# The third MoE span by seven products, and five PSUM copies given to VectorE

## The chip, the cores and the metric

The kernel runs on one core of one Trainium2 chip. The metric is the device time of one execution in microseconds (us), from the start of the program on the core to its end. Several timed executions are made and their median is taken. Beside them stands one profiled execution, from which every duration of a single instruction in this document comes.

The core's engines work from instruction queues of their own, each in order: TensorE (PE in the profile, its weight loads apart as PEld), VectorE (DVE), ScalarE (ACT), GpSimd (POOL) and SyncE (SP), which here issues DMAs. They wait for one another through semaphores.

## The reference

The kernel computes a blockwise causal attention and feeds its result to a small MoE block with a maximum of two projections as its activation. Cut to what matters:

```python
B, H, S, D = 8, 8, 576, 64
scores = (1/sqrt(D)) * q @ k^T            # masked in blocks of 64, block_i >= block_j
attn   = softmax(scores)
x      = (attn @ v) as [B*S, H*D]         # 4608 tokens x 512
h1, h2 = x @ w1, x @ w2                   # 512 -> 1024
out    = maximum(h1, h2) @ w_out          # 1024 -> 512, float32, 4608 x 512
```

The kernel uses max(h1, h2) = h2 + relu(h1 - h2). With d = w1 - w2, g = relu(x @ d) and M = w2 @ w_out, the output is y = x @ M + g @ w_out. So a row block of y is a sum over twelve chunks of 128: four of x against M and eight of g against w_out.

## The kernel before, in words

**Attention.** The 64 heads are taken in 32 pairs `p`, two pairs to a group `g` and four pairs to a batch of 576 tokens. For a pair, TensorE makes scores (L536, L554) into PSUM, ScalarE takes the exponential into SBUF (L560, L616), GpSimd zeroes the masked corners (L565), and TensorE multiplies by v (L644, tile `ps_o`). VectorE divides by the sum (reciprocal L650, multiplication L651 into `xp`). The result is transposed into `xT`, from the third batch on by a DMA transpose issued by SP (L662). K is cast by a GpSimd DMA (`kb`, L138) and transposed by another DMA of SP (L147, `kT`), from group 6 on; q is loaded by SP (L121), cast on GpSimd (L161), transposed on TensorE (L517) and copied out of PSUM, one head pair by VectorE and the other by ScalarE (L525).

**MoE.** The tokens are cut into ten spans: two small ones for the first batch, then spans 2 to 9 of 512 tokens (the last 448). Per span, eight units (`h_unit`) make x @ d for 128 of the 1024 columns, with four matmuls of 512 columns each (L244), and `g` is written by the relu. In spans below `FAST` VectorE does every relu (L252); from `FAST` on ScalarE does the odd ones (L250).

Then y is made in one of two ways:

- Spans below `FAST` (0, 1 and 2) use `y_unit`: for each 128 tokens, twelve matmuls of 512 columns into one bank of PSUM (L291), one VectorE copy out (L296), one store of SP (L297). Span 2 has four such units, 48 matmuls.
- Spans from `FAST` on use seven products in place of eight half-size ones, a scheme of Strassen's kind. A span is two row halves of 256 tokens, x|g is cut into two halves of the twelve chunks, and the weights M|w_out into two column halves of 256. Sums of halves are formed first: `weight_sums` (L354, eight instructions in all, once per kernel) and `row_sums` (L360, eight per span). A product is twelve matmuls of 256 columns (L386, tile `ps_p`), so a span has 84. `after` combines the products: the first is copied out of PSUM to a tile `u` (L411, on ScalarE), the others are added by VectorE (L415, L420, L426, L431, L435, L437, L440). SP stores the four quarters (L405).

The order of the products is (1, 2, 6, 5, 4, 7, 3) for all spans but the last one.

**What sets the order.** The order of every engine's instructions is written out by hand: instructions are issued in the order in which the Python code runs, and each engine takes its own in that order. MoE work is cut into generators (`units`), and `fill(n)` issues about n matmuls' worth of it between pieces of attention. Which unit comes next is decided by order in the list and by whether the tokens it needs are done (`done_tokens`). `fill_of(g)` spreads the ready work evenly over the groups. The main loop runs over groups, with two pairs each, and each pair does: MoE work, attention of pair p-2 in two parts around a few matmuls (`av_with`: `ps_o` of two tiles, fill, `ps_o` of three tiles), transposes of q, scores of the next tiles, GpSimd work, then one `weight_sums` for p = 10 to 17.

**PSUM.** The scores have four banks of eight. Everything else (`ps_h`, `ps_y`, `ps_p`, `ps_o`, `ps_qT`) shares the other four, in pool `ps_m`: a matmul that opens a new tile waits until the former tile in its bank has been read. In the steady groups the bank of product 1 goes next to the three-tile `ps_o` that follows the second product.

Of the kernel before, what the change touches and what calls it, by code (L numbers as in the profile page):

```python
# [14 lines left out]
def kernel(  # L15
# [57 lines left out]
    NSPAN = len(spans)  # L73


    FAST = 3
    carry = [t0 % P for t0, _ in spans]
    tiles = [(carry[i] + w) // P for i, (_, w) in enumerate(spans)]

# [31 lines left out]
    dve, pool, act = nc.vector.tensor_copy, nc.gpsimd.tensor_copy, nc.scalar.copy  # L111
# [88 lines left out]
    dve, pool, act = nc.vector.tensor_copy, nc.gpsimd.tensor_copy, nc.scalar.copy  # L200
# [30 lines left out]
    def h_unit(i, f):  # L231
# [11 lines left out]
        for c in range(NDM):  # L243
# [4 lines left out]
            if c == NDM - 1:  # L248
                if i >= FAST and on_act(i, f):
                    nc.scalar.activation(out=g[:, f, m:m + w], in_=pt[:, :w], func=AF.Relu)  # L250
                else:
                    nc.vector.tensor_scalar_max(g[:, f, m:m + w], pt[:, :w], 0.0)  # L252
                if i >= FAST and f in X_SUMS:
                    row_sums(i, X_SUMS[f], 0)
            yield

    def bT_unit(j):
        pt = ps_m.tile([P, 2, NDM, P], BF16, name="ps_bT", tag="m")
        for i in range(2):
            for c in range(NDM):  # L260
                nc.tensor.transpose(pt[:, i, c, :], w2_sb[j][:, c, i * P:(i + 1) * P], ident[:])
                if i == 1 and c == NDM - 1:
                    (act if j % 2 else dve)(
                        out=bT_sb[:, 2 * j:2 * j + 2, :],
                        in_=pt.rearrange("p i c d -> p i (c d)"))
                yield
# [65 lines left out]
    def b_parts(half, col):  # L332
        cs = slice(col * HN, (col + 1) * HN)
        return m_sb[:, 2 * half:2 * half + 2, cs], wo_sb[:, 4 * half:4 * half + 4, cs]

    def t_parts(n):
        return slot[n][:, 0:2], slot[n][:, 2:6]
# [8 lines left out]
    def weight_sums(n):  # L346
        m, op, x, y = (
            (1, sub, (0, 1), (0, 0)), (3, sub, (1, 1), (0, 1)),
            (2, add, 3, (0, 0)), (4, sub, (1, 0), 2))[n // 2]
        if not slot:  # L350
            for k in range(1, 5):
                slot[k] = wraw.tile([P, 8, HN], BF16, name="sums", tag="w1raw")
        get = lambda z: b_parts(*z) if isinstance(z, tuple) else t_parts(z)
        op(t_parts(m)[n % 2], get(x)[n % 2], get(y)[n % 2])  # L354

    def row_sums(i, n, k):
        op, x, y = (
            (add, (1, 0), (1, 1)), (sub, 1, (0, 0)), (sub, (0, 0), (1, 0)), (sub, (0, 1), 2))[n - 1]
        get = lambda z: a_parts(i, *z) if isinstance(z, tuple) else s_parts(i, z)
        op(s_parts(i, n)[k], get(x)[k], get(y)[k])  # L360
# [8 lines left out]
    def on_act(i, f):  # L369
        return i >= 8 or f % 2  # L370

    def product(i, n, cuts=((0, 0, HN), (1, 0, HN))):
        for m in G_SUMS.get(n, ()):
            row_sums(i, m, 1)
        lhs = chunks({1: lambda: a_parts(i, 0, 0), 2: lambda: a_parts(i, 0, 1), 4: lambda: a_parts(i, 1, 1)}.get(
            n, lambda: s_parts(i, {3: 4, 5: 1, 6: 2, 7: 3}[n]))())
        rhs = chunks({1: lambda: b_parts(0, 0), 2: lambda: b_parts(1, 0), 3: lambda: b_parts(1, 1)}.get(
            n, lambda: t_parts({4: 4, 5: 1, 6: 2, 7: 3}[n]))())
        st = part_sums.setdefault(i, {})
        pt = None  # L380
        for k, (s, m, w) in enumerate(cuts):
            if pt is None or len(cuts) > 2:
                pt, p0 = ps_m.tile([P, 2 * HN if len(cuts) == 2 else w], FP32, name="ps_p", tag="m"), s * HN + m
            q0 = s * HN + m - p0
            for c in range(6):
                nc.tensor.matmul(  # L386
                    pt[:, q0:q0 + w], lhs[c][:, s * P:(s + 1) * P], rhs[c][:, m:m + w],
                    start=(c == 0 and q0 == 0), stop=(c == 5 and q0 + w == pt.shape[1]),
                )
                if c == 5 and q0 + w == pt.shape[1]:  # L390
                    after(i, n, st, pt, p0, q0 + w)
                yield

    def after(i, n, st, pt, p0, w):
        new = lambda: y_pool.tile([P, d_model], FP32, name="y")
        t0 = spans[i][0] - carry[i]

        def store(t, row, col):
            r0 = t0 + 2 * row * P
            if w < d_model:  # L400
                s, m = divmod(p0, HN)
                nc.sync.dma_start(
                    out=out[r0 + s * P:r0 + (s + 1) * P, col * HN + m:col * HN + m + w], in_=t[:, p0:p0 + w])
                return
            nc.sync.dma_start(  # L405
                out=out[r0:r0 + 2 * P, col * HN:(col + 1) * HN].rearrange("(s p) d -> p s d", p=P),
                in_=t.rearrange("p (s d) -> p s d", s=2))

        if n == 1:
            st["u"] = new()  # L410
            act(out=st["u"][:], in_=pt[:])  # L411
        elif n == 2:
            if i < NSPAN - 1:
                st["c"] = new()
                add(st["c"][:], pt[:], st["u"][:])  # L415
            else:
                add(st["c"][:, p0:p0 + w], pt[:], st["c"][:, p0:p0 + w])
            store(st["c"], 0, 0)
        elif n == 6 and i < NSPAN - 1:
            add(st["u"][:], pt[:], st["u"][:])  # L420
        elif n == 6:
            st["c"], st["u"] = st["u"], new()
            add(st["u"][:], pt[:], st["c"][:])
        elif n == 5:
            st["v"] = new()
            add(st["v"][:], pt[:], st["u"][:])  # L426
            if 4 in st:
                add(st["u"][:], st[4][:], st["u"][:])
        elif n == 4:
            if "v" in st:  # L430
                add(st["u"][:], pt[:], st["u"][:])  # L431
            st[4] = pt
        elif n == 7:
            t = new()
            add(t[:], pt[:], st["v"][:])  # L435
            store(t, 1, 1)
            add(st["u"][:], pt[:], st["u"][:])  # L437
            store(st["u"], 1, 0)
        elif n == 3:
            add(st["v"][:], pt[:], st["v"][:])  # L440
            store(st["v"], 0, 1)
# [6 lines left out]
    def plan():  # L448
        def h(i, f):
            t0, w = spans[i]  # L450
            units.append((h_unit(i, f), t0 + w, w / SPAN, NDM))

        def y(i, s, last=False):
            t0, w = spans[i]
            if last:
                units.append((y_last(i, s), t0 + w, 0.333, 3 * NY))
            else:
                units.append((y_unit(i, s), t0 + w, 1.0, NY))

        for i in range(NSPAN):  # L460
            for f in range(NFF):
                h(i, f)
                if i > FAST and f < 7:
                    units.append((product(i - 1, ORDER[f]), spans[i - 1][0] + spans[i - 1][1], 0.5, NY))
                if i == 0 and f % 2:
                    units.append((bT_unit(f // 2), 0, 0.25, 2 * NDM))
                if 2 < i <= FAST and f % 2 == 0 and f // 2 < tiles[i - 1]:
                    y(i - 1, f // 2)
# [230 lines left out]
    def fill_of(g):  # L699
        if g == NG - 1:  # L700
            return 45
        left = 5 - g if g < 5 else 2 - (g - 5) % 2
        return -(-max(0, ready() - KEEP) // left)
# [146 lines left out]
    for g in range(GPB + 1, NG):  # L850
        a, b = 2 * g, 2 * g + 1
        old = done_tokens[0]
        if x_due:
            x_out(x_due.pop())
        n, new = fill_of(g), done_tokens[0]
        region(tile_0(a), tile_1(a))
        lo, hi = max(3, n // 18), n * 2 // 9
        for p, tiles in ((a, lambda: (tile_2(a), tile_0(b))), (b, lambda: (tile_1(b), tile_2(b)))):
            done_tokens[0] = old if p == a and x_by_dma(g - 2) else new
            fill(hi)  # L860
            av_with(p - LAG, lo)
            done_tokens[0] = new
            if p % 2 and x_by_dma(g - 1):
                x_dma(g - 1)
            if p % 2 == 0:
                for nm in "qk":
                    if g + 1 < NG and by_dma(nm, g + 1):
                        transpose_blocks(nm, g + 1)
            copy_out = t_pair(p)
            outs = tiles()  # L870
            copy_out()
            region(*outs)
            if p % 2 and g + 1 < NG:
                pad_keys(p + 1)
                pad_keys(p + 2)
            pool_work(p)
            if 0 <= p - 10 < 8:
                weight_sums(p - 10)
        x_due.append(g - 1)
        fill(n - 2 * (lo + hi))  # L880
    for p in range(NPAIR - LAG, NPAIR):
# [48 lines left out]
```

## Time and profile before

| | |
|---|---|
| median of 3 timed executions | 253.36 us (253.33 to 253.37) |
| profiled execution: its time | 254.14 us |
| its span, first to last instruction | 252.2 us |
| PE busy | 238.7 us, 95% |
| DVE busy | 172.1 us, 68% |
| ACT busy | 143.4 us, 57% |
| POOL busy | 129.3 us, 51% |
| granted TensorE clock | 1.00 throughout |

The profiled execution takes 0.78 us more than the median, and 1.94 us of it lie around the span. Differences are worked out within it and then applied to the median.

In the middle of the kernel the work repeats once per batch (two groups). In the trace such a stretch runs from one block of five `ps_h` matmuls to the next: 70.60 to 96.06 us (the stretch in which y of span 2 is made), 96.06 to 121.32, 121.32 to 146.58, 146.58 to 171.84 (spans 3, 4 and 5), and 171.84 to 195.68 us (span 6, with less attention left to prepare). In the timeline, a row is one group of like instructions: start, duration to the end of the last one, engine, line, tiles, count, and in brackets how long the engine stood idle before it and what released it. Matmuls overlap: a row's duration has the tail of its last matmul in it, so the distance between the starts of two rows tells the pace.

### The profile page before, as it was taken

How to read it: one execution, taken by the hardware profiler on the slowest of the kernel's cores; microseconds unless marked ns; L12 is line 12 of the kernel's file. 1: busy time of each engine (PE TensorE's matmuls, PEld its weight loads, DVE VectorE, ACT ScalarE, POOL GpSimd, SP SyncE). 2: the span in 40 equal slices, each digit the busy share in tenths (PEclk: the TensorE clock that was granted, in tenths of full speed). 3: DMA queues.
4: the chain of work that ended last, by engine and by line, in shares of the span. 5: the costliest groups of instructions: out<-in, count | busy, mean ns of one | idle time of the engine just before them, and what ended most of it. 6: DMA issues, size and time to landing. Idle time of an engine off the chain costs nothing.

```text
span 252.2 us, 7449 instructions
## 1 busy us (share of the span) xinstructions
PE 238.7 (95%) x3037; PEld 160.2 (64%) x3037; DVE 172.1 (68%) x371; ACT 143.4 (57%) x200; POOL 129.3 (51%) x294
## 2 busy tenths in 40 slices
PE   8699899799999999999999999999999999999992
PEld 2347667656555555577657765776578568567782
DVE  4876986657496638786678567856785788526573
ACT  2788864575673738673867386748674650362200
POOL 1996952479759385938493849384622220010000
PEclk9999999999999999999999999999999999999999
DMA  7999999579899999999999899999993321301205
GB/s 241 317 220 310 192 270 225 215 61 198 176 134 251 158 187 171 213 111 185 246 217 157 162 208 114 203 138 220 156 154 70 109 55 44 125 0 44 91 34 170
DMA packets 107842, 41.32 MB, mean 164 GB/s; under 512 B 89248, under 2 KB 100640, under 8 KB 107808
## 3 DMA queue, kind: packets, MB, share of 16 engines
q0 software_dynamic: 65952, 11.87, 61.6%
q1 hardware_dynamic: 41584, 28.39, 50.7%
q8 instruction: 24, 0.39, 0.8%
q10 hardware_dynamic: 272, 0.59, 0.7%
q14 instruction: 10, 0.08, 0.1%
HBM read 34.60 MB, written 9.44 MB: 175 GB/s over the span
## 4 chain that ended last, share of the span: by engine, by line
PE 71%; ACT 10%; DMA 6%; DVE 6%; POOL 3%; issue 2%; SPq 0%; ACTq 0%; DVEq 0%; POOLq 0%
PE ps_p L386 21%; PE ps_h L244 19%; PE ps_y L291 9%; PE ps_o L644 8%; PE ps_s L536 7%; ACT aT L560 6%; PE ps_w L506 4%; DMA kraw<-in_k_dram 4%; DMA qraw<-in_q_dram 3%; DVE bT_sb L360 2%; ACT g L250 2%; PE ps_qT L517 2%; PE ps_M L272 1%; POOL kn L161 1%; DVE y L435 1%
## 5 line engine op out<-in xcount | busy, mean ns | idle before, releaser
L560 ACT ACTIVATE aT<-ps_s 128x1024 bf16<-128x1024 f32 (+2 forms) x100 | 95.7, 994 | 35.4 <-PE ps_s L536 26.3
L244 PE MATMUL ps_h<-xT,d_sb 128*128 128x512 bf16 (+3 forms) x320 | 69.4, 358 | 0.3 <-DVE d_sb L191 0.3
L565 POOL MEMSET aT<- 64x128 bf16 x124 | 22.0, 200 | 58.3 <-ACT aT L560 57.3
L244 PEld LDWEIGHTS <-d_sb 128*128 128x128 bf16 x320 | 29.5, 98 | 27.3 <-issue 2.3
L644 PEld LDWEIGHTS <-aT 128*128 128x128 bf16 x960 | 37.2, 98 | 10.9 <-issue 3.1
L644 PE MATMUL ps_o<-vv,aT 128*128 128x65 bf16 x960 | 39.8, 194 | 1.6 <-ACT y L411 1.6
L252 DVE TENSOR_SCALAR g<-ps_h 128x512 bf16<-128x512 f32 (+2 forms) x44 | 26.4, 605 | 13.6 <-PE ps_h L244 13.1
L165 POOL DMA_DIRECT2D vv<-in_v_dram x40 | 33.9, 854 | 1.3 <-issue 0.9
L250 ACT ACTIVATE g<-ps_h 128x512 bf16<-128x512 f32 (+1 forms) x36 | 20.9, 586 | 23.2 <-PE ps_h L244 22.3
L651 DVE TENSOR_TENSOR xp<-ps_o,rec 128x256 bf16<-128x256 f32 (+1 forms) x64 | 31.4, 491 | 2.2
L536 PE MATMUL ps_s<-qT,kT 64*128 64x64 bf16 (+6 forms) x344 | 31.3, 280 | 1.6 <-ACT kT L525 0.7
L138 POOL DMA_DIRECT2D kb<-in_k_dram x40 | 29.4, 758 | 0.0
L386 PE MATMUL ps_p<-sums,bT_sb 128*128 128x256 bf16 x168 | 25.2, 273 | 0.0
L525 ACT COPY qT<-ps_qT 128x576 bf16<-128x576 bf16 (+1 forms) x17 | 10.3, 614 | 24.6 <-PE ps_qT L517 24.6
L386 PEld LDWEIGHTS <-bT_sb 128*128 128x128 bf16 x224 | 21.4, 98 | 3.4 <-issue 1.0
L650 DVE RECIPROCAL rec<-ps_o 128x4 f32<-128x4 f32 (+1 forms) x64 | 11.8, 184 | 15.1 <-PE ps_o L644 15.1
L161 POOL CAST qn<-qraw 128x1152 bf16<-128x1152 f32 (+1 forms) x16 | 17.2, 1072 | 8.7 <-DMA qraw<-in_q_dram 8.7
L536 PEld LDWEIGHTS <-kT 64*128 64x128 bf16 x344 | 12.2, 94 | 10.7 <-issue 5.0
L386 PEld LDWEIGHTS <-g 128*128 128x128 bf16 x172 | 15.6, 98 | 3.5 <-issue 1.9
L386 PE MATMUL ps_p<-wo_sb,g 128*128 128x256 bf16 (+1 forms) x116 | 17.6, 269 | 0.0
L291 PE MATMUL ps_y<-wo_sb,g 128*128 128x512 bf16 x64 | 16.7, 380 | 0.0
L236 POOL COPY g<-g 128x512 bf16<-128x512 bf16 x8 | 5.9, 732 | 20.6 <-ACT g L250 20.3
(94 smaller groups left out, 317.9 us busy)
## 6 DMA issues: line engine op xcount, KB each, us to landing
qraw<-in_q_dram SPq DMA_DIRECT2D x16, 576.0 KB, 5.2
out_dram<-y SPq DMA_DIRECT2D x35, 256.0 KB, 3.7
vv<-in_v_dram POOLq DMA_DIRECT2D x32, 128.0 KB, 6.1
kraw<-in_k_dram SPq DMA_DIRECT2D x5, 576.0 KB, 7.7
kb<-in_k_dram POOLq DMA_DIRECT2D x40, 72.0 KB, 6.9
w1raw<-in_moe_w_dram POOLq DMA_DIRECT2D x4, 512.0 KB, 7.4
xT<-in_moe_w_dram POOLq DMA_DIRECT2D x4, 256.0 KB, 7.9
wo_sb<-in_moe_w_out_dram POOLq DMA_DIRECT2D x2, 512.0 KB, 9.8
```

The costliest lines, as they stand in the source:

```text
L138: nc.gpsimd.dma_start(out=n[h * BLK:(h + 1) * BLK, :, s], in_=(q if nm == "q" else k)[b, 4 * u + 2 * s + h].rearrange("(j p) d -> p j d", ...
L165: nc.gpsimd.dma_start(out=vv_r[b % NV][P - rows:, c, :, :D], in_=v[b, :, c * P:c * P + rows, :].rearrange("h p d -> p h d"),)
L244: nc.tensor.matmul(pt[:, :w], d_sb[:, c, f * P:(f + 1) * P], xT[:, c, t0:t0 + w], start=(c == 0), stop=(c == NDM - 1),)
L250: nc.scalar.activation(out=g[:, f, m:m + w], in_=pt[:, :w], func=AF.Relu)
L252: nc.vector.tensor_scalar_max(g[:, f, m:m + w], pt[:, :w], 0.0)
L291: nc.tensor.matmul(py[:], lhs, rhs, start=(n == 0), stop=(n == len(terms) - 1),)
L386: nc.tensor.matmul(pt[:, q0:q0 + w], lhs[c][:, s * P:(s + 1) * P], rhs[c][:, m:m + w], start=(c == 0 and q0 == 0), stop=(c == 5 and q0 + w ...
L536: nc.tensor.matmul(ps[:, hh, col:col + w], kT[r, k0:k0 + P], qT[r, q0:q0 + w], start=True, stop=True,)
L560: nc.scalar.activation(out=aT_r[p % NA][:, :, a0:a0 + w], in_=ps[:, :, :w], func=AF.Exp, scale=scale,)
L565: (eng or nc.gpsimd).memset(aT_r[p % NA][BLK:, :, a0:a0 + BLK], 0.0)
L644: nc.tensor.matmul(po[:, gi, hh, :], a[:, hh, a0:a0 + P], vv[:, c, h0 + 2 * hh, :], start=(mm == 0), stop=(mm == n_mm - 1),)
L651: nc.vector.tensor_mul(xp[:, :, ts[0]:ts[0] + n, p % 2].rearrange("q s t d -> q t s d"), po[:, :, :, :D], rec[:, :n].to_broadcast([P, n, 2 ...
```

## The change

There are three edits, all in the order and placement of work; the output is the same sums.

1. `FAST` goes from 3 to 2, so span 2 is done as the later spans: y by seven products (84 matmuls of 256 columns in place of 48 of 512), the odd relus on ScalarE, eight `row_sums` and eight combining instructions on VectorE (one copy, seven additions) in place of four copies and four relus.
2. `weight_sums` is called twice per pair at p = 8 to 11, in place of once per pair at p = 10 to 17, so that the sums exist when span 2 needs them.
3. The copy of the first product out of PSUM is issued to VectorE in place of ScalarE for spans 2 to 6; for spans 7 to 9 it stays on ScalarE.

```diff
-    FAST = 3
+    FAST = 2
...
         if n == 1:
             st["u"] = new()
-            act(out=st["u"][:], in_=pt[:])
+            (dve if i < 7 else act)(out=st["u"][:], in_=pt[:])
...
             pool_work(p)
-            if 0 <= p - 10 < 8:
-                weight_sums(p - 10)
+            for i in range(2 * (p - 8), 2 * (p - 8) + 2):
+                if 0 <= i < 8:
+                    weight_sums(i)
```

In the changed program TensorE's instructions in span 2's stretch stand in the same order as in the stretches of spans 3, 4 and 5. Outside that stretch TensorE's order is as before. On VectorE the copy (L411) stands after the copy of qT (L525) and ahead of the reciprocal (L650) of the next two-tile `ps_o`. On SP the four stores of span 2 are quarters of 256 x 256 in place of 128 x 512.

## The prediction

> **What bounds the kernel now.** I read the page first: TensorE is busy for 95% of the span and carries most of the chain of waits that ended last. The question is then where TensorE stands still.
>
> ```profile
> PE 238.7 (95%) x3037; PEld 160.2 (64%) x3037; DVE 172.1 (68%) x371; ACT 143.4 (57%) x200; POOL 129.3 (51%) x294
> PE 71%; ACT 10%; DMA 6%; DVE 6%; POOL 3%; issue 2%; SPq 0%; ACTq 0%; DVEq 0%; POOLq 0%
> ```
>
> Second, the busy time by stretch: span 2's stretch (y by whole units), then those of spans 3, 5 and 6 (y by products).
>
> ```profile
> 70.60:96.06 25.46, 25.46 (x293) 13.59 (x292) 16.43 (x35) 14.03 (x19) 16.82 (x38) 1.00 1.63 185
> 96.06:121.32 25.26, 24.62 (x329) 17.23 (x328) 19.66 (x41) 16.76 (x24) 16.79 (x38) 1.00 1.79 171
> 146.58:171.84 25.26, 24.62 (x329) 17.25 (x328) 18.09 (x37) 16.73 (x24) 16.78 (x38) 1.00 1.43 164
> 171.84:195.68 23.84, 23.44 (x307) 16.48 (x306) 16.54 (x35) 15.61 (x22) 10.15 (x27) 1.00 1.15 151
> ```
>
> The first numbers are length and PE busy. Span 2's stretch has no idle TensorE at all; each later one is only 0.20 us shorter and has 0.64 us of idle in it. Third, the list of waits tells which idle that is; of TensorE's own waits in these stretches only the first and the third row are there.
>
> ```profile
> PE ps_o L644 <- ACT y L411: 1.6, 4, 0.4
> DVE y L415 <- ACT y L411: 1.4, 4, 0.4
> PE ps_qT L517 <- DVE xp L651: 0.7, 3, 0.2
> ```
>
> Fourth, the timeline around one of the four, for TensorE, ScalarE and VectorE.
>
> ```profile
> 160.22 0.38 PE L386 MATMUL ps_p<-sums,xsum 128*128 128x256 bf16 x2
> 161.00 0.90 PE L644 MATMUL ps_o<-vv,aT 128*128 128x65 bf16 x24 [0.40 <-ACT y L411]
> ...
> 159.45 1.02 ACT L560 ACTIVATE aT<-ps_s 128x1024 bf16<-128x1024 f32 x1
> 160.37 0.58 ACT L411 COPY y<-ps_p 128x512 f32<-128x512 f32 x1
> ...
> 158.68 0.75 DVE L525 COPY qT<-ps_qT 128x576 bf16<-128x576 bf16 x1
> 159.98 0.18 DVE L650 RECIPROCAL rec<-ps_o 128x4 f32<-128x4 f32 x1 [0.55 <-PE ps_o L644]
> 160.20 0.42 DVE L651 TENSOR_TENSOR xp<-ps_o,rec 128x256 bf16<-128x256 f32 x1
> 160.98 0.69 DVE L415 TENSOR_TENSOR y<-ps_p,y 128x512 f32<-128x512 f32 x1 [0.36 <-ACT y L411]
> ```
>
> Product 1 is complete at 158.88 (its last matmul starts at 158.60 and takes 0.27), but its copy stands on ScalarE behind two exponentials and starts at 160.37. The three-tile `ps_o` needs that bank. Two matmuls after 160.22, at a pace of 0.11, TensorE could have begun it at 160.44; it began at 161.00. So the stall is 0.56 us, not the 0.40 of the row, which counts from the tail of the last matmul. It is the same in the stretches of spans 3, 4, 5 and 6. By the same reading the third wait, before the transposes of q, costs 0.43 (begun at 169.75, second matmul at 170.18, where such matmuls follow one another in hundredths).
>
> Fifth, the pace of the two sorts of y matmuls.
>
> ```profile
> 86.48 1.90 PE L291 MATMUL ps_y<-wo_sb,g 128*128 128x512 bf16 x8
> 88.22 1.03 PE L291 MATMUL ps_y<-m_sb,xT 128*128 128x512 bf16 x4
> 89.08 1.46 PE L291 MATMUL ps_y<-wo_sb,g 128*128 128x512 bf16 x6
> ```
>
> From 86.48 to 89.08 are 12 matmuls: 0.217 each. In span 5's stretch the 28 matmuls of 256 columns from 162.41 to 165.48 take 0.110 each.
>
> **The change, part by part.**
>
> Edit 1, span 2 by products. TensorE: 48 x 0.217 = 10.4 us go, 84 x 0.110 = 9.2 come: 1.2 us less. The rest of the stretch stands in the order of the later ones, so it gets their 0.43 stall before the transposes (VectorE works through two additions of product 7, a reciprocal and a multiplication first): net -0.76. With the 0.56 stall too it would be -0.20, which is just the 25.46 against 25.26 of the table; the sum reproduces the stretches.
> VectorE in that stretch: four copies (0.69) and four relus (0.69) go; eight row sums (0.41 to 0.86), one copy and seven additions (0.69) come. That is span 5's load, 18.09 us of 25.26, plus about 2 us of sums. ScalarE gets four relus of 0.60: as in span 5, whose ScalarE waits for TensorE (0.48 to 1.72 us) before each pair of exponentials. Both lie beside TensorE; without that cover a relu late on ScalarE would hold a `ps_h` bank for 0.60.
>
> Here the Trainium skill has a rule against the edit. "TensorE: Matmul & The Clock Gate", section "Back-to-back issue gap", gives sustained spacings of 81 ns for 128 columns and 131 ns for 512. On a straight line that makes an estimated 98 ns for 256: 84 products' matmuls would take 8.2 us against 6.3, a loss of 1.9 in place of a gain of 1.2, and the whole change would end 0.1 us slower. The trace does not show these spacings: its rows give 110 and 217 ns, half the columns at half the time, and the measurement decides.
>
> Edit 2, the weight sums. The same eight instructions (0.41 or 0.68), two more at p = 8 and p = 9 each, and the last ones earlier. At p = 8 they start behind the copy of qT, at 59.30, and take about 0.93 at VectorE's pace; VectorE stood idle for 0.97 there until 60.34. At p = 9 the idle is 2.04 (63.2 to 65.23). At p = 10 the larger sum is new ahead of the copy of the last `ps_y`: the copy ends at 72.04 in place of 71.43, and its bank is wanted at 72.35. At p = 11 one smaller sum is new, ahead of a relu: 0.1 late, nobody waits. Cost taken: 0. The bounds: 0, and 0.8 if the sums at p = 10 ran at half pace, as the row sum at 153.14 does (0.86 in place of 0.41) while GpSimd casts q; GpSimd sets masks at that place, and the wide sums' rows are all 0.68. A gain is excluded, since no sum was waited for. Span 3's stretch loses 1.8 us of sums (19.66 against 18.09 busy); VectorE is not what ends there.
>
> Edit 3, the copy on VectorE. No row shows VectorE copying `ps_p`, but `ps_y` has the same form: 0.69, against ScalarE's 0.58. Hand over span 5: product 1 ready at 158.88, VectorE free of the qT copy at 159.35, copy until 160.04. TensorE wants the bank at 160.44: 0.40 to spare, the 0.56 stall goes. Queued behind the copy are the reciprocal and multiplication of the two-tile `ps_o`. They start at 159.98 as before, since the copy is issued in the 0.55 of idle and the pace between such instructions is 0.61. Then L415 can start at 160.55 in place of 160.98, so everything behind is earlier too. VectorE also takes over the wait for a free `y` buffer; that store was issued a stretch earlier and lands within 2 to 8 us. ScalarE loses 0.58 and only idles more. What is late next: the scores after `ps_o`, now at 161.27, need exponentials that end at 160.47; then `kT` (below).
> Gain: four stretches x 0.56 = 2.24.
>
> Queues. GpSimd issues the same DMAs and masks in the same order. On SP, span 2's four stores have the old size but stand where later spans have theirs, so the transposes of `kT` come behind the pair of stores after product 7: 1.5 us before the next block of `ps_h` (144.88 against 146.42) in place of 3.2 (92.88 against 96.06). TensorE needs `kT` 8.2 us after that issue (153.07 less 144.88). At this place the transposes landed after 5.2, 5.3 and 7.8 us; the longest of all took 9.3. Cost between 0 and (9.3 - 8.2) x 5 = 5.5 us. I take 0: three rows at this very place held. The third is close: its weight load waited 0.4 us, without holding a matmul up. A gain is excluded; no matmul waits for `kT` now.
>
> The sum: -0.76 - 2.24 = -3.00. Against the profiled execution: span 252.2 to 249.2, its time 254.14 to 251.14. That execution is 0.78 over the median, so the median goes from 253.36 to 250.36.
>
> **The rivals.**
>
> A. The copy comes late on VectorE as well, and the bank's stall stays under another name. Against it: 0.40 us to spare in a stretch whose instructions repeat to a hundredth. For it: VectorE is nearly gapless from 155.5 to 164.4, so a copy late by 1 us finds no room. With all five stalls at 0.56: 253.36 - 0.20 = 253.16, within 0.2%.
>
> B. DMA sets the pace of the stretch. For it: the DMA engines are 90% busy or more in most slices, 1.4 to 1.8 packets in flight per engine. Were each stretch held half way, -3.00 would become -1.50: 251.9. Against it: landings of 2.6 us for the transposes of x at 138 and 189 show that the backlog clears.
>
> C. Slower: the transposes of `kT` land after TensorE wants them, at the one place above, once per stretch. At the longest landing, 9.3, five stalls of 1.1 cost 5.5 and eat the 3.0: 255.9. It decides from a mean landing of 8.8 us on (0.6 of stall in each of five). For it: 2% more DMA per time, and the 7.8 row. Against it: the 5.2 and 5.3.
>
> D. The seven products do not save what the pace says, the bank's stall goes all the same: -2.24 and the new 0.43, 251.6.
>
> **How the numbers follow.** The forecast, within 0.5 of 250.4: 0.70. B or D, 251 to 252.8: 0.15. A: 0.06. C, or some other wait of VectorE that I did not see: 0.09. The upper end goes to 252.0, which takes in B and D; the lower to 249.8, since nothing but the 0.43 stalls could still go. Outside lie A, C and the worst of B, about 0.18. A measurement of this kernel can tell about 0.2% (0.5 us) from no change; faster than that: 0.70 + 0.15 = 0.85; the same: 0.06; slower: 0.09.
>
> **What would show it.** Right: the waits of `ps_o` for L411 are gone from the list; the five stretches take 24.7 us each (span 6's 23.3), with the 0.43 before the transposes in the first four as TensorE's only idle; 48 fewer `ps_y` matmuls, 84 more `ps_p`. Wrong: `ps_o` waiting for L411 on VectorE (A); weight loads or scores waiting for `kT` (B, C); the stretch of span 2 gaining less than 0.5 (D); a reciprocal that starts later after its `ps_o` than before, with `ps_qT` waiting longer.

## The result and the profile after

The changed kernel takes 250.34 us in the median (249.97 to 251.42, four executions), the kernel before, on the same chip, 253.37 us (253.33 to 253.55). The ratio is 0.9886, with a 95% interval of 0.9854 to 0.9918. In a second set of measurements (shown below as an experiment) it was 0.9877, 0.9858 to 0.9896. The forecast was 250.4 us.

The profiled execution took 251.42 us, with a span of 249.6 us. Busy time of the engines and the chain of waits that ended last, of the kernel after:

```profile
PE 234.7 (94%) x3054; PEld 163.8 (66%) x3073; DVE 179.1 (72%) x383; ACT 143.7 (58%) x200; POOL 128.9 (52%) x294
PE 79%; DMA 9%; DVE 4%; POOL 3%; ACT 2%; issue 1%; SPq 0%; POOLq 0%
```

TensorE has 4 us less to do, VectorE 7 us more, and ScalarE's part of the chain falls from 10% to 2%. The chain's DMA part grows by 5.8 us; 5.4 of them are a load of q at the start of the program, where the chain of the profile before took another path.

The stretches of the kernel after, of spans 2, 3 and 5 (length; busy time of PE, PEld, DVE, ACT, POOL; clock; DMA share; GB/s):

```profile
70.91:95.61 24.70, 24.41 (x329) 17.25 (x328) 20.43 (x43) 16.28 (x23) 16.76 (x38) 1.00 1.64 177
95.61:120.31 24.70, 24.35 (x329) 17.24 (x328) 18.55 (x38) 16.25 (x23) 16.75 (x38) 1.00 1.66 183
145.01:169.71 24.70, 24.35 (x328) 17.23 (x328) 18.55 (x38) 16.25 (x23) 16.75 (x38) 1.00 1.46 190
```

All are 24.70 us long, and span 2's stretch now has the 329 matmuls of the others. Measured alike in both traces, from the first block of `ps_h` matmuls of a span to the first block of the next, the five stretches of spans 2 to 6 take

| stretch of span | 2 | 3 | 4 | 5 | 6 | sum |
|---|---|---|---|---|---|---|
| before | 25.45 | 25.26 | 25.27 | 25.26 | 24.56 | 125.80 |
| after | 24.70 | 24.70 | 24.70 | 24.70 | 24.00 | 122.80 |

So -3.00 us between 70 and 196 us. (The stretches given ahead of the prediction begin 0.16 us behind the block's first matmul, and the last of them was ended at 195.68, where no block begins: the next one starts at 196.24. So span 6's stretch is 24.56 and not 23.84, and the 24.00 here stands against the 23.3 of the prediction.) The list of waits of the kernel after has no row of `ps_o` behind L411 any more; TensorE's row for the transposes of q behind `xp` has one occurrence more, and the early one behind the cast of q, at 47 us, is larger than the 1.3 of before:

```profile
PE ps_qT L517 <- POOL qn L161: 1.8, 1, 1.8
...
PE ps_qT L517 <- DVE xp L651: 1.0, 4, 0.2
```

That early wait is why the span of this one execution fell by 2.6 us and not by 3.0.

The timeline around the place where the stall was, now in span 2's stretch, for TensorE and then for VectorE:

```profile
83.87 0.38 PE L386 MATMUL ps_p<-m_sb,xT 128*128 128x256 bf16 x2
84.09 0.35 PE L644 MATMUL ps_o<-vv,aT 128*128 128x65 bf16 x6
84.27 0.60 PE L386 MATMUL ps_p<-wo_sb,g 128*128 128x256 bf16 x4
84.71 0.38 PE L386 MATMUL ps_p<-sums 128*128 128x256 bf16 x2
84.93 0.90 PE L644 MATMUL ps_o<-vv,aT 128*128 128x65 bf16 x24
```

```profile
83.17 0.75 DVE L525 COPY qT<-ps_qT 128x576 bf16<-128x576 bf16 x1
83.84 0.68 DVE L411 COPY y<-ps_p 128x512 f32<-128x512 f32 x1
84.47 0.18 DVE L650 RECIPROCAL rec<-ps_o 128x4 f32<-128x4 f32 x1
84.69 0.42 DVE L651 TENSOR_TENSOR xp<-ps_o,rec 128x256 bf16<-128x256 f32 x1
85.03 0.68 DVE L415 TENSOR_TENSOR y<-ps_p,y 128x512 f32<-128x512 f32 x1
```

And the same place in span 5's stretch, the one that the prediction shows with its stall:

```profile
158.81 0.38 PE L386 MATMUL ps_p<-sums,xsum 128*128 128x256 bf16 x2
159.03 0.90 PE L644 MATMUL ps_o<-vv,aT 128*128 128x65 bf16 x24
```

In span 2's stretch the copy of product 1 stands right behind the copy of qT and ends at 84.52. The three-tile `ps_o` starts at 84.93, two matmuls after 84.71, with no idle time in brackets; in span 5's stretch it is 0.22 as well (159.03 less 158.81). The reciprocal follows the copy without a gap, 0.03 us after the modelled end of its `ps_o` (84.44).

What is left of TensorE's idle time in a stretch, in the same kernel:

```profile
93.67 0.20 PE L517 MATMUL ps_qT<-ident,qn 64*128 64x64 bf16 x1
94.11 0.43 PE L517 MATMUL ps_qT<-ident,qn 64*128 64x64 bf16 x17 [0.24 <-DVE xp L651]
```

From the first transpose of q to the second are 0.44 us, where others follow in hundredths: VectorE has not yet freed the bank, behind two additions of product 7.

### The profile page after: what moved, and what is told of

The parts are those of the page before. It is cut to its first block, busy times and chain, and to the rows that moved or that the text cites. A ratio compares the mean times of both kernels' runs of the same rounds, so it can differ in the third digit from the quotient of the medians.

```text
span 249.6 us, 7510 instructions
## 1 busy us (share of the span) xinstructions
PE 234.7 (94%) x3054; PEld 163.8 (66%) x3073; DVE 179.1 (72%) x383; ACT 143.7 (58%) x200; POOL 128.9 (52%) x294
## 4 chain that ended last, share of the span: by engine, by line
PE 79%; DMA 9%; DVE 4%; POOL 3%; ACT 2%; issue 1%; SPq 0%; POOLq 0%
PE ps_p L386 29%; PE ps_h L244 22%; PE ps_o L644 9%; PE ps_s L536 9%; DMA qraw<-in_q_dram 5%; PE ps_y L291 4%; DMA kraw<-in_k_dram 4%; PE ps_qT L517 2%; PE ps_M L272 1%; ACT aT L560 1%; DVE y L435 1%; DVE y L437 1%; POOL kn L161 1%; PE ps_w L506 1%; DVE xp L651 1%
## 5 line engine op out<-in xcount | busy, mean ns | idle before, releaser
L244 PE MATMUL ps_h<-xT,d_sb 128*128 128x512 bf16 (+3 forms) x308 | 68.4, 357 | 1.0 <-DVE d_sb L191 0.3
L250 ACT ACTIVATE g<-ps_h 128x512 bf16<-128x512 f32 (+1 forms) x40 | 23.3, 587 | 23.4 <-PE ps_h L244 22.1
L252 DVE TENSOR_SCALAR g<-ps_h 128x512 bf16<-128x512 f32 (+2 forms) x40 | 23.6, 596 | 12.8 <-PE ps_h L244 12.5
L386 PE MATMUL ps_p<-sums,bT_sb 128*128 128x256 bf16 x192 | 28.9, 273 | 0.0
L386 PEld LDWEIGHTS <-bT_sb 128*128 128x128 bf16 x256 | 24.4, 98 | 3.9 <-issue 1.2
L525 ACT COPY qT<-ps_qT 128x576 bf16<-128x576 bf16 (+1 forms) x17 | 10.3, 614 | 24.5 <-PE ps_qT L517 24.5
L386 PEld LDWEIGHTS <-g 128*128 128x128 bf16 x196 | 17.7, 98 | 4.1 <-issue 2.4
L386 PE MATMUL ps_p<-wo_sb,g 128*128 128x256 bf16 (+1 forms) x132 | 20.1, 270 | 0.0
L650 DVE RECIPROCAL rec<-ps_o 128x4 f32<-128x4 f32 (+1 forms) x64 | 11.8, 184 | 9.7 <-PE ps_o L644 9.5
L360 DVE TENSOR_TENSOR bT_sb<-g 128x1024 bf16<-128x1024 bf16 x16 | 11.0, 689 | 6.6 <-ACT g L250 6.0
```

The lines of the kernel that those rows point to most:

```text
L244: nc.tensor.matmul(pt[:, :w], d_sb[:, c, f * P:(f + 1) * P], xT[:, c, t0:t0 + w], start=(c == 0), stop=(c == NDM - 1),)
L386: nc.tensor.matmul(pt[:, q0:q0 + w], lhs[c][:, s * P:(s + 1) * P], rhs[c][:, m:m + w], start=(c == 0 and q0 == 0), stop=(c == 5 and q0 + w ...
```

## The experiments

Stretches are given as in the table above, for spans 2 to 5. "Early wait" is the time that TensorE loses at about 46 us, before the transposes of q of group 4, measured by the pace like the other stalls.

**1. The copy alone.** The kernel before, with the third edit only.

```diff
-            act(out=st["u"][:], in_=pt[:])
+            (dve if i < 7 else act)(out=st["u"][:], in_=pt[:])
```

> Edit 3 alone: span 2 by whole units and the weight sums as before, the first product of spans 3 to 6 copied by VectorE. My theory: the four stalls of 0.56 us before the three-tile ps_o go and nothing else moves, so the stretches of spans 3, 4 and 5 take 24.7 us in place of 25.26, that of span 2 stays at 25.46, and the time is 253.37 - 2.24 = 251.1 (ratio 0.991). Rival A (the copy is late on VectorE too): 253.4. If the gain of the whole change came from the seven products: 253.4.

Measured: 251.18 us (250.61 to 252.11), ratio 0.9933 (0.9915 to 0.995). Stretches 25.46, 24.70, 24.70, 24.69, and span 6's 24.00: 0.56 less in each of four, nothing in span 2's. No wait of `ps_o` for L411 is left. The third edit by itself is worth 4 x 0.56 = 2.24 us in the trace. The ratio of the timed executions gives 1.7 us (1.3 to 2.2), somewhat less.

**2. Span 2 by products, the copy left on ScalarE** (edits 1 and 2).

```diff
-    FAST = 3
+    FAST = 2
...
-            if 0 <= p - 10 < 8:
-                weight_sums(p - 10)
+            for i in range(2 * (p - 8), 2 * (p - 8) + 2):
+                if 0 <= i < 8:
+                    weight_sums(i)
```

> Edits 1 and 2 without 3: span 2 by seven products, the copy on ScalarE in all spans. My theory: TensorE saves 1.19 us of matmuls in span 2's stretch but gets both stalls of the later stretches there (0.56 and 0.43), so that stretch goes from 25.46 to 25.26 and the time from 253.37 to 253.2 (ratio 0.999). If the seven products alone were worth the change: 250.3. If matmuls of 256 columns cost more than half of those of 512, as the spacings of the skill's page on TensorE would have it: 255 to 256.

Measured: 252.88 us (252.35 to 255.0), ratio 1.0002 (0.9985 to 1.002). Stretches 25.27, 25.25, 25.26, 25.27. The waits of this kernel:

```profile
PE ps_o L644 <- ACT y L411: 2.0, 5, 0.4
...
PE ps_qT L517 <- DVE xp L651: 0.9, 4, 0.2
```

There are now five stalls behind ScalarE's copy and four behind `xp`. In span 2's stretch the products save 1.2 us and bring back 0.56 and 0.43: 25.45 becomes 25.27, too little for the times to show. The first edit pays only because the third removes the stall that it would inherit: alone it is worth 0.2 us, on top of the copy 0.76.

**3. The weight sums alone** (edit 2: their earlier and denser order, with `FAST` left at 3).

> Edit 2 alone: the weight sums two per pair from p = 8, all else as before. My theory: hidden in idle time of VectorE, 253.4, ratio 1.000, and no new wait of TensorE. Rival (VectorE's queue is what ends the pairs of group 4): up to 2.2 us slower, 255.6.

Measured: 252.96 us (252.03 to 253.47), ratio 0.9992 (0.9979 to 1.0004), stretches 25.46, 25.26, 25.26, 25.27. The sums cost nothing that can be seen.

**4. The copy twice.** The changed kernel, with VectorE's copy issued two times.

```diff
         if n == 1:
             st["u"] = new()
+            if i < 7:
+                dve(out=st["u"][:], in_=pt[:])
             (dve if i < 7 else act)(out=st["u"][:], in_=pt[:])
```

> The changed kernel with the VectorE copy of the first product issued twice (same source and target) in spans 2 to 6, which doubles its cost and nothing else. My theory: the single copy ends 0.40 us before TensorE wants the bank, the second ends 0.60 to 0.68 later, so each of the five stretches gets a stall of 0.20 to 0.28 and the time goes from 250.3 to 251.4-251.8. If the copy had no slack: five times 0.6, 253.4. If it had more than 0.7: 250.3.

Measured: 251.91 us (251.1 to 252.9), ratio 0.9953 (0.9936 to 0.997), stretches 25.08, 25.08, 25.08, 25.09. The timeline of span 5's stretch, VectorE and TensorE:

```profile
157.19 0.68 DVE L411 COPY y<-ps_p 128x512 f32<-128x512 f32 x1
157.91 0.69 DVE L413 COPY y<-ps_p 128x512 f32<-128x512 f32 x1
...
158.06 0.38 PE L386 MATMUL ps_p<-sums,xsum 128*128 128x256 bf16 x2
158.65 0.91 PE L646 MATMUL ps_o<-vv,aT 128*128 128x65 bf16 x24 [0.21 <-DVE y L413]
```

The second copy starts 0.72 us after the first, not 0.61; that it waits because it writes the same tile is likely, but not shown. `ps_o` could have begun at 158.28 and began at 158.65: a stall of 0.37 in each of five stretches, somewhat more than expected, since the delay was 0.72. The other 0.35 is what the copy really had to spare (I had read 0.40). This is rival A brought about on purpose: the bank's stall returns under VectorE's name as soon as the copy is later than that.

**5. The 0.43 stalls taken away as well.** ScalarE copies product 7, and VectorE's two additions of it, with their stores, come after the third relu unit of the next span.

```diff
         elif n == 7:
             t = new()
+            if i < 7:
+                act(out=t[:], in_=pt[:])
+
+                def finish(u=st["u"], v=st["v"]):
+                    add(u[:], t[:], u[:])
+                    store(u, 1, 0)
+                    add(t[:], t[:], v[:])
+                    store(t, 1, 1)
+                later.append(finish)
+                return
...
-            add(st["v"][:], pt[:], st["v"][:])
-            store(st["v"], 0, 1)
+            z = new() if i < 7 else st["v"]
+            add(z[:], pt[:], st["v"][:])
+            store(z, 0, 1)
...
             if c == NDM - 1:
+                if f == 2 and later:
+                    later.pop()()
```

> The changed kernel with product 7 of spans 2 to 6 copied out of PSUM by ScalarE, and its two additions on VectorE moved behind the third relu unit of the next span (from SBUF; product 3's sum gets a tile of its own). My theory: the 0.43 us stall before the transposes of q is VectorE working through those two additions ahead of the reciprocal; with them gone it vanishes in the four stretches that have it, which then take 24.27 us, and the time falls from 250.3 to 248.6. Rival (VectorE has no room for 1.2 us of additions later, or the store of u comes too late for the next span's tile): 250 to 253.

Measured: 249.21 us (248.59 to 249.55), ratio 0.9844 (0.9823 to 0.9865). Stretches 24.27, 25.14, 24.27, 24.27: three gain the 0.43, and span 3's loses 0.44, through a wait that was not there before. TensorE, then SP's queue, in this kernel:

```profile
112.10 0.38 PE L390 MATMUL ps_p<-sums,xT 128*128 128x256 bf16 x2
113.30 0.61 PE L551 MATMUL ps_s<-qT,kT 64*128 64x512 bf16 x6 [0.82 <-DMA kT<-kb]
```

```profile
102.64 0.97 SPq L409 DMA_DIRECT2D out_dram<-y  x2
103.78 3.73 SPq L147 DMA_TRANSPOSE kT<-kb  x2
```

The scores could have begun at 112.42, 0.32 after the row before (in the kernel after, the same two rows start at 89.40 and 89.72); they began at 113.30, held for 0.88 by `kT`. Its two transposes were issued behind the two deferred stores and landed 9.5 and 9.3 us after their issue. In experiment 7, the changed kernel, the first of them was issued at 102.31 and landed at 109.82; here it was 103.78 and 113.25. So of 3.43 us that it came later, 1.47 are the later issue and 1.96 a longer time to landing. This is the mechanism of rival C, in one of the stretches, and at another pair of transposes than the pair after product 7's stores that the prediction had named. The median is 0.6 above the 248.6 of the theory.

**6. The copy on VectorE in all spans**, 7 to 9 too.

```diff
-            (dve if i < 7 else act)(out=st["u"][:], in_=pt[:])
+            dve(out=st["u"][:], in_=pt[:])
```

> The changed kernel with the copy of the first product on VectorE in all spans, 7 to 9 too. My theory: after the last attention pairs no matmul waits for that copy, on either engine, so nothing changes: 250.3, within 0.3. Rival (what helps is VectorE as such, everywhere): 0.56 less per span, 248.7. Rival (VectorE is full in the tail): later by up to 0.6 per span, 252.

Measured: 249.70 us (249.53 to 253.27), ratio 0.9897 (0.9862 to 0.9933), all stretches as in the changed kernel, 24.70. The median is 0.3 below that of experiment 7, which was measured with it. The end of the program, from span 9's first `ps_h` matmul on, took 28.78 us against 29.02 and 29.06 in the two traces of the changed kernel, but TensorE's part of it, from that matmul to its last one, is 24.57 in all three. So no difference can be seen that comes from which engine copies there.

**7. The changed kernel again**, unaltered.

> The changed kernel itself once more, with more rounds on one chip. From its own and the first four experiments' traces, the stretches from span 2 on give 3.0 us less than before (ratio 0.988). The start of the kernel, up to the first transposes that wait for the load of q, differs from run to run by up to 1.4 us in the traces, so single times will scatter by that much while the stretches stay at 24.7.

Measured: 249.97 us (249.77 to 250.18), ratio 0.9877 (0.9858 to 0.9896), span 248.0, stretches 24.70 four times. The span is 1.6 us shorter than in the first profile, and the difference lies ahead of span 2: the early wait is 0.65 in place of 1.83, and a load of q lands at 44.47 us in place of 46.10 (more on it in experiment 12).

**8. The deferred stores on ScalarE's queue.** As 5, but the additions and the stores are two steps; the stores come after the fifth relu unit and are issued by ScalarE, out of the way of SP's transposes.

```diff
-                if f == 2 and later:
-                    later.pop()()
+                if f in (2, 4) and later:
+                    later.pop(0)()
...
-                def finish(u=st["u"], v=st["v"]):
+                def sums(u=st["u"], v=st["v"]):
                     add(u[:], t[:], u[:])
-                    store(u, 1, 0)
                     add(t[:], t[:], v[:])
-                    store(t, 1, 1)
-                later.append(finish)
+
+                def stores(u=st["u"]):
+                    store(u, 1, 0, nc.scalar)
+                    store(t, 1, 1, nc.scalar)
+                later.extend((sums, stores))
```

> As the run with the deferred additions (ScalarE copies product 7, VectorE adds it after the third relu unit), but the two stores that belong to these additions are issued by ScalarE's queue after the fifth relu unit, so that SP reaches the transposes of kT without them, as in the changed kernel (there issued at 102.31 and 103.71, landed by 109.8 and 111.7). Theory (the 0.88 us at 113.30 came from kT being issued 1.5 to 2.5 us later behind these two stores): no TensorE wait for kT; the four 0.43 us stalls before the transposes of q stay away; every one of the first four stretches takes 24.27 to 24.37, against 24.37, 25.15, 24.27, 24.27 with the stores on SP and 24.81, 24.70, 24.70, 24.70 in the changed kernel; span about 0.9 us under the former at the same early wait, median 248.2 to 248.6. Rival (the landing was late for DMA traffic, not for the place on SP): a wait of 0.5 us or more for kT stays in one of the stretches, median about 249.2. Second rival (two issues on ScalarE hold back the exponentials behind them): a new wait of ps_o or ps_s for ScalarE of 0.3 us or more per stretch, median 249.5 or more.

Measured: 249.3 us (248.07 to 250.58), ratio 0.9826 (0.9787 to 0.9866). Stretches 24.27, 24.27, 25.38, 24.26. The wait for `kT` and the 0.43 stalls are gone, as the theory had it, and TensorE waits nowhere for ScalarE after 60 us, against the second rival. The median is above the 248.2 to 248.6 of the theory. But span 4's stretch has a new wait, for a load of v:

```profile
141.85 0.34 PE L661 MATMUL ps_o<-vv,aT 128*128 128x65 bf16 x6 [0.95 <-DMA vv<-in_v_dram]
```

```profile
132.60 0.69 POOL L165 DMA_DIRECT2D vv<-in_v_dram  x1
```

It was issued at 132.60 and landed at 141.81, 9.2 us later; in experiment 7 the load at this place took 4.7.

**9. The same kernel again.**

> The same kernel as the run with the deferred stores on ScalarE's queue, a second time. There one TensorE wait of 1.12 us was new, for a load of v that landed 9.2 us after its issue (4.7 in the changed kernel). If the DMA backlog decides (rival B of the prediction, at a shorter stretch): a wait for some load, of v, kT or q, stands again in one of the first five stretches, maybe at another place and of another size, and the times scatter over more than 1 us again; median 248.8 to 249.6. If that wait was a single event: all first four stretches 24.27 to 24.37 and a median of 248.2 to 248.6.

Measured: 248.34 us (247.92 to 250.64), ratio 0.983 (0.9798 to 0.9863), span 246.2. Stretches 24.27, 24.26, 24.27, 24.27, and no wait for a load after 50 us. The wait for v did not come back in this profile; a smaller one of its kind is in experiment 12. The scatter of the times stayed at 2.7 us, and experiment 12 looks for its place.

**10. Half of the stores left out**, in the kernel of 8.

```diff
+            if 2 <= i < 7:
+                q.dma_start(out=out[r0:r0 + P, col * HN:(col + 1) * HN], in_=t[:, :HN])
+                return
```

> As the run with the deferred stores on ScalarE's queue, but spans 2 to 6 store only the first of each pair's two halves: 2.6 MB less of the output is written (5 spans x 4 stores x 128 KB), so the output lacks these rows; computation and order stay. If the DMA backlog is what makes loads late once the stretches are shorter: no TensorE wait for kT, v or q after 50 us, first four stretches 24.27 to 24.37, landings of the transposes of kT back to 5 to 7.5 us from 9 to 10, median 248.0 to 248.6 and a scatter of the runs below 1 us. If loads are late for another reason (an issue that is late on its queue): the 1.1 us wait for v, or one for kT, stays; median 249.3 as there.

Measured: 248.8 us (248.02 to 251.5), ratio 0.9841 (0.9804 to 0.9877). The stretches are 24.27, 24.26, 24.27, 24.27, as in 9 with all stores. The transposes of `kT` between 72 and 175 us land after 4.8 to 9.4 us, median 7.8; in 9 it was 4.9 to 9.2 and 7.5. So the bytes of the stores are not what makes these landings long, and the expectation that they return to 5 to 7.5 us was wrong. The median and the scatter (3.5 us, for less than 1) missed as well. What makes them long in the kernels with deferred additions (medians 7.3 to 7.8, against 6.2 and 6.5 in the two traces of the changed kernel, and 7.1 in the kernel before), stays open.

**11. Half of the stores left out, in the changed kernel.** The same edit, on SP's queue.

> The changed kernel with the same halved stores in spans 2 to 6 (the output lacks these rows). It tells whether DMA traffic costs the changed kernel anything. If it doesn't: stretches 24.81, 24.70, 24.70, 24.70, 24.00 as with all stores, median 249.7 to 250.4 (249.97 in both sets of runs with all stores lies in it). If traffic holds it back: some stretch falls below 24.65 or the median below 249.4.

Measured: 250.92 us (249.92 to 253.66), ratio 0.9901 (0.9879 to 0.9923). Not faster than with all stores, and in the trace the stretches are 24.71, 24.70, 24.70 and 24.70. The transposes of `kT` land sooner (5.8 us in the median, for 6.2 and 6.5), but TensorE had not waited for them. Traffic of the stores costs these stretches nothing, against rival B. The median is above the expected range; what made the profiled execution the longest, 253.66, is told in experiment 12, and the others left no trace.

**12. Twelve matmuls of M ahead of the early wait**, in the kernel of 8.

```diff
-            fill(hi)
+            fill(hi if g > GPB + 1 else (2 * hi if p == a else 0))
```

> The deferred additions with their stores on ScalarE's queue, and in the third pair of heads (about 42 to 50 us) the 12 matmuls of m_sb that stand after the transposes of q are done before them: 12 x 0.110 = 1.3 us of work that is due anyway, while the load of q is still under way. In the eleven traces so far TensorE waits there for that load, for 0.16 to 2.4 us, and the two profiles in which it stood idle for over 2.0 us at that place also show a granted clock of 0.68 and 0.50 in the 4 us after it and some 1.7 us more time. Theory (the scatter of all these kernels sits in that wait): the wait falls by 1.3 us, in most runs to nothing; no run shows the low clock; the runs scatter by under 0.8 us, median 247.6 to 248.2 (248.34 and 249.3 without the edit); the stretches from 68 us on stay at 24.37, 24.27, 24.27, 24.27. Rival (the scatter has another place, before 42 us or after 190 us): scatter of 2 us as before, median 248.3 to 249.3. Second rival (the wait only moves, to the transposes of k or to the exponentials, which now come 1.3 us later): a new TensorE wait of 0.5 us or more between 46 and 56 us, median 248.3 or more.

Measured: 248.83 us (248.07 to 250.06), ratio 0.9818 (0.9789 to 0.9846), stretches 24.27, 24.44, 24.27, 24.27. The 0.17 in span 3's stretch is a load of v again: it landed at 117.70, 8.3 us after its issue, and the 24 matmuls of a `ps_o` take 1.07 us in place of 0.90, going on at 117.74. So with the stalls gone this kernel is near its loads of v; two of its traces show such a wait. The early wait did not go, it was 1.48 us in this profile, and 0.46 for an exponential came new at 51.63 (the second rival, in part). The median is above the forecast, and the scatter is 2.0 us. To see why, one has to set the landing of the load of q beside the start of span 2's first `ps_h` block, over nine of the fourteen traces (the difference is 24.79 or 24.80 in the other five):

| trace | load of q lands | early wait | first `ps_h` block | difference |
|---|---|---|---|---|
| experiment 4 | 44.22 | 0.40 | 69.02 | 24.80 |
| experiment 9 | 44.25 | 0.43 | 69.05 | 24.80 |
| experiment 7 | 44.47 | 0.65 | 69.27 | 24.80 |
| experiment 8 | 44.91 | 1.18 | 69.71 | 24.80 |
| before | 45.63 | 1.38 | 70.44 | 24.81 |
| after | 46.10 | 1.83 | 70.91 | 24.81 |
| experiment 10 | 46.00 | 2.14 | 72.44 | 26.44 |
| experiment 11 | 46.56 | 2.20 | 73.01 | 26.45 |
| experiment 12 | 46.84 | 1.48 | 70.80 | 23.96 |

The theory on the place holds: the start of span 2 hangs on that load, to 0.01 us in this table for one order of instructions at the full clock, and its landing differs by 2.6 us between the profiled executions. Part of that is there before the load: it was issued between 38.25 and 39.80 us. In experiment 12 it came latest of all; the edit gains 0.84 us after it (24.80 less 23.96: 1.3 less the new 0.46). The size was wrong, because the edit doesn't touch the scatter of the landing itself. Why the loads of the first 45 us land so differently stays open.

Experiments 10 and 11 have 1.64 us more on top. TensorE's granted clock tells what that is, in windows of 2 us (clock third from the end), first experiment 10, then the kernel after:

```profile
46.00:48.00 2.00, 0.68 (x28) 0.53 (x28) 0.28 (x2) 0.17 (x1) 1.50 (x2) 1.00 0.62 230
48.00:50.00 2.00, 2.00 (x16) 1.42 (x13) 0.97 (x2) 1.95 (x4) 1.49 (x5) 0.68 0.10 36
50.00:52.00 2.00, 2.00 (x18) 1.56 (x17) 1.03 (x3) 0.74 (x1) 0.74 (x2) 0.50 0.00 0
52.00:54.00 2.00, 2.00 (x59) 1.63 (x57) 1.07 (x3) 0.63 (x2) 1.22 (x2) 0.97 0.80 51
```

```profile
48.00:50.00 2.00, 2.00 (x27) 1.59 (x22) 1.41 (x3) 1.95 (x4) 1.57 (x5) 1.00 0.18 65
50.00:52.00 2.00, 2.00 (x60) 1.71 (x57) 1.22 (x5) 1.00 (x2) 0.65 (x2) 1.00 0.00 0
```

After the longer wait the clock in the three rows from 48 us on falls short of full by 0.64, 1.00 and 0.06 us, 1.70 together. That is 3.4 us at half the clock, and about the 1.64.

## Why the prediction was right, point by point

- **The sum.** -3.00 was forecast for the middle of the kernel, and the five stretches give -3.00. The median came to 250.34 and 249.97 us, for 250.4. That it lies as near as that is partly luck, since the first four executions spread over 1.45 us; it is the stretches that repeat well enough to show the -3.00. In the profiled execution, where 249.2 and 251.14 were forecast, it is 249.6 and 251.42. The difference lies ahead of the change: the load of q behind the early wait landed 0.47 us later than in the profile before, which the prediction had not counted as something that differs between executions.
- **Edit 1.** -0.76 was forecast with the bank's stall gone, and -0.20 with it. Span 2's stretch went from 25.45 to 24.70 in the changed kernel (-0.75) and to 25.27 in experiment 2 (-0.18). The pace of 0.110 per matmul of 256 columns holds: four such matmuls span 86.34 to 86.78 in the trace after. So the loss that the Trainium skill's spacings ("TensorE: Matmul & The Clock Gate", section "Back-to-back issue gap") would give did not come. Rival D falls too. VectorE's load was forecast at about 20.1 us, measured 20.43. One row sum ran slower than the bound I gave: 1.08 us under GpSimd's cast, against 0.41 to 0.86.
- **Edit 2.** Cost 0, and experiment 3 shows 0. At p = 10, where it was closest, the wide sum took 0.68 (no half pace), the last copy of `ps_y` started at 71.82, and the next `ps_o` at 72.82, without idle time.
- **Edit 3.** 4 x 0.56 were forecast and experiment 1 shows 0.56 in each of the four stretches. The 0.40 to spare is 0.35 by experiment 4; a copy 0.72 later brings a stall of 0.37 (rival A).
- **What is late next.** Only the 0.43 before the transposes is left in a stretch, as forecast, and experiments 5, 8 and 9 take it away.
- **The queues.** The cost of 0 for the transposes of `kT` was right: they landed after 3.3 to 8.5 us in the profile after and 3.5 to 8.0 in experiment 7, and TensorE waited for none. Of the prediction's figures for them one is read with a mixed mark: from 92.88 to the block's first matmul it is 3.0 us (95.89), not 3.2. The mechanism of rival C is real, though the prediction looked for it at one pair of transposes alone. Experiment 5 brings it about at the other pair, with a landing of 9.5 us behind two more stores, at 0.88 us in one stretch, so the kernel is not far from it. Rival B had no part in these stretches (experiment 11).

## What to carry to other kernels

Two edits of a change can be worth little and much: span 2's products alone gained 0.2 us, and 0.76 once the copy had taken the stall away that the new order would have inherited; add the stalls of the order that a stage moves into before counting its saving. A stall is measured by the pace of the matmuls around it, not by the idle time in its row (0.56 against 0.40 here), and the slack of a fix is measured by making the fix later on purpose. When work is put off to clear one engine, look at what its DMA issue then stands in front of: two stores ahead of a transpose, and its longer time to landing, cost one stretch twice what the deferral had gained in it (0.88 us against 0.43, in one profile).

## What the runs showed of the hardware that was not expected

The landing of one load carries most of the difference between the traces of one kernel. It lies between 44.22 and 46.84 us in the fourteen traces (the DMA engines moved 370 to 388 GB/s from 44 to 46 us in the profiles after and of experiments 10 to 12), and from there to the first `ps_h` block of span 2 the time repeats to 0.02 us in a given order of instructions and at the full clock. What else differs are single late loads (experiments 8 and 12), the clock, and the time from TensorE's last matmul to the end of the span, 3.84 to 4.74 us. Executions that were only timed left no trace, so that their scatter has the same places is likely, but not shown. A comparison of two kernels by stretches is therefore good to some 0.02 us, where no load comes late in them, while their times scatter by 1 us and more.

A short idle time of TensorE goes with a drop of its clock. In the two profiles in which TensorE stood still for 2.07 and 2.13 us at 46 us (by the brackets of the rows), the clock in the records fell to 0.50 some 1.4 and 0.9 us after it had work again, and came back after 3.4 us. In the other twelve, with at most 1.76 us of idle time there, it stayed at 1.00. The Trainium skill, "TensorE: Matmul & The Clock Gate", section "Part 1: The HAM clock gate (the "warmup" mystery)", has a gate that halves the clock after an idle window of about 3.4 us and frees it after a busy one. The half clock and its length agree with these rows; an idle time of 2.07 us was enough here, though. Where between 1.76 and 2.07 us it sets in, and whether the windows' phase decides, was not tried.
